# First two token groups of an attention + two-MLP kernel: passes with rounded weights first, passes with their rests second, and a new written order

## The chip, the cores and the metric

The kernel runs on one core of one Trainium2 chip. The metric is the device time of one launch in microseconds (us). Five engines run side by side, each through its own list of instructions in order: TensorE (PE: matmuls), VectorE (DVE), ScalarE (ACT), GpSimd (POOL) and SyncE (SP, which here issues every transfer). They wait for each other through semaphores only.

## The reference, cut to what matters

```python
attn_out = softmax(where(s >= max(s) - tau, s, -1e9)) @ v       # s = q k^T / 8; 4 x 8 heads, 576 x 64
x = attn_out.transpose(0, 2, 1, 3).reshape(2304, 512)
h = x @ w_in                                                     # 512 -> 2048
g = (a0 + a1 h + a2 h^2 + a3 h^3) / (1 + |b0||h| + |b1|h^2 + 1e-6)
y = g @ w_out                                                    # 2048 -> 512
out = ((y @ w1) * (y @ w2) @ w3) @ w_out2                        # 512 -> 1024 -> 1024 -> 512
```

All inputs and the output are float32, and `moe_b` is scaled up by 47.694.

## The kernel before, in words

**Tiling.** Tokens are worked on in 18 groups of 128: group n < 16 is block n % 4 of batch n // 4, groups 16 and 17 hold the last 64 rows of two batches each. Attention goes by batch b, head pair c and 128-row block (`qk`, `top`, `thr`, `exp`, `recip`, `p_norm`, `p_hi`, `p_lo`, `p_t`, `pv`, `x_split`). `p_t` is a transposing transfer through SP, and `pv` multiplies its result with V.

**Split numbers.** A float32 operand of the MLPs is carried as two float16 numbers: the rounded number (the first half of a tile) and the rest that the rounding left (the second half). A product takes three passes for each of its four weight pieces, in the code (0,0), (0,1), (1,0): rounded times rounded, and each rounded number times the other's rest. So a product of 128 tokens with 512 columns is 12 matmuls of 128x512, issued in two halves of 6: pieces 0 and 1, then pieces 2 and 3. The four products are `h_product` (w_in), `y_product` (w_out), `ab_product` (w1, w2) and `o_product` (W = w3 @ w_out2, made once by `w_product`).

**Weight preparation.** Each of 72 raw tiles of 512 KB is loaded (`raw_w`) into one of three `wr` buffers, turned into float32 words in two steps (`conv_w`: the head by any engine, then a shift and an or on DVE, which frees the buffer), squared on ACT for a norm (`square_w`, `norm_w`), and split: `split_w` writes the rounded piece from ACT, DVE or POOL, PE makes the rest in PSUM (two matmuls against `dg`, one against `minus`), and ACT or DVE copies it out.

**Scales.** `limits` loads tau and derives the factor of q and the threshold; `powers` loads the coefficients a and b and takes a logarithm and an exponential of one number on ACT; `setup` selects the one table of ACT functions that holds everything the kernel needs, and sets a few constants.

**The order.** All events (2533 calls like "qk of batch 0, head pair 1, block 2") are made into generators. `ORDER` is a long string of 3944 tokens that says which generator is advanced next, on which engine its copy runs (a for ACT, p for POOL, v or nothing for DVE), and into which buffer numbers its tiles go. Every engine's list of instructions follows from that string, and nothing is reordered later. The line in the loop is `if gens[n] is not None: next(gens[n], None)`, so each `yield` in a function is a place where other work can come between.

**Names that the prediction uses.** L410 to L434: `limits` and `powers`; L398: the table of `setup`; L451, L452, L408, L670: loads of q, k, tau and weights; L681: second step of `conv_w`; L512/L507: `qk`; L521: `top`; L359: `thr` and the like; L543/L548: `exp`; L599: `pv`; L688/L691: squares; L697: `norm_w`; L733/L734: the matmuls that make a rest; L809: `h_product`; L930: `w_product`.

Of the kernel before, what the change touches and what calls it, by code (L numbers as in the profile page):

```python
# [32 lines left out]
52.0 36.1 0 38a.0 38.0 14.0.1 1 15v 54p.1 54.1 8.0 3 23.0.1 28.2 2 25.0 27 29v.0 31.0.2 33.3 33a  # L33
31a 30a.0 30.2 4.1 51.1.0 5.0.0 35a 48.0 50p.1 35 37v 45v.4 10.1 6.2 7.1 50.3 53.1 55 9.0 44.2 47
11.1 12 12.0 12 84a.0.0 19.5.6 46p.0 46.4 21a 84 32.0 86.7.8 57v.1 34v.1 34.5 16.2 13v.1.1 13 20.0
40.1 49.0 59.1.0 62.1 18v.0 39v.3 88a 18.6 24.2 41p 152a.2.2 62a 152 59a 64a 64 90.0.1 74a.2 22v.1
66a 92.2 94 42a.0 76 96p.2 68p.4 98.2.1 70p 43.1 78 22.7 61.0 56.1 26v.1 98a 100.0 100a 119.0.1
26.8 72 56 75.2 63p.1 42.9 102a 102 113v.3 115 121.3 56 123 125a.0 104a 107v.2 127.3.5 127a 129.6
129a 63.10 65.1 103.0 80.0.0 109v 82v 77a.0 77.11 158.0.1 56 82 111.0 116.2 117.1 118a.1 160.0
67p.0 67.12 162 164v.1 131v 131 141v.0 133v 58v.13 105p.0 166.4.4 154.1.2 166a 143 69.0 105.14  # L40
118.15 69 168.6 17v.3.3 17 69 168a 170a 135a.3 156p 186.0.1 188.1 137v 170 180a.7 106.1 69 190
79.0 81v.0 108v.1 81.16 120.2 71a.17 172v 139 108.18 174v.8 145 192p.2 195.5.5 132.0 83.1 197.3
122v.0 83 182 93.1 184.2 195a 122.19 621.2 176v 147.0 149v 149 197a 223.0.1 199p 199 225.2 201v
203a.0 134p.1 134.20 89.0 227 229v.0 95a.0 178.0 95.21 205p 91v.1 231.6.6 231a 83 83 110.0 110
233.4 233a 252.0.1 91.22 254.3 110 171.1 85a.23 219.7.5 221p 97.1 209v.8 256 97 97 97 288 647.0
650p.0 136.0 624v.1 235p 624.24 258v.1 641.2 173a.1 211 260.7.1 262.2 173.25 262a 235 645v.1
246a.3 213 124.1 650.26 110 99v.27 260a 237v 163.0 290.1.0 645.28 112v.29 652.1 126p.0 291.0
165v.1 126.30 293 295a.2 297.0.8 297a 207 298.0 298a 148.2 165.31 150p.0 613.0 140.1 613 142a.1
628.0 150.32 264p 179.2 248 630p.0 264 300v 652 314.1.0 316.1 142.33 613 652 250.1 613 318 300
630.34 319p.0 321.1.4 321a 240v.5 242v 210.1 212p.1 339.1 302a 266v 274v.3 155.0 616a.35 309a.6  # L50
276 181v.0 212.36 181.37 633.0 114.1 311 284.7.2 633 157a.1 268v.0 157.38 278 619.1 128.1 304a.3
341.2 342v.1 218.1 220p.0 305v 323.8 270v 194.2 196p.1 633 633 636a.39 652 323a 187.0 344.2.1
220.40 226.1 196.41 215.0 217v 234.2 655a.42 189p.0 130.1 60.1 344v 346p 217 325a 144.1 286a
189.43 228p.1 236p.0 202.0 365 138 151.0 325 326v 146 159.1 153 153 167.0 161.0 169 191.1 228.44
193.1 204p.1 183.0 241.1 236.45 244.0 175.1 177 185 185 367.0.1 312.2 198.1 200 327.2 204.46 206.0
346 369.3 370 272 333v.5 335 208 243p.0 222.1 224.0 230.0 238.1 313.0 243.47 328p.6 330p 372v.2
320.1 232 239 214.0 216 216 245.1 247 247 249 249 329p.1 374.3.8 251p.0 267v.48 376.4 263v.49 376a
348a 349p.0 315p.0 255a.50 265a.51 253a.52 280.1 253.0 257a.53 337 329.54 259v.55 281a.56 374a
438.0 438 277a.3 659.0 282v 315.1 255.1 255a 285.2 438 438 377p 261a.10 391.1.0 438 253a 287a.1
257.1 377 393.0 259.0 307.0 287.12 257a 277.1 382.0 73.1 259a 332 282 267.0 351p 269p.11 386v.5  # L60
379a 322v.0 283a.16 277a 395 397v.0 441.0 267a 271v.14 398.4.1 400.2 638.0 322.22 261.1 292.2
362.3.6 398v 385p.1 388 261a 385.21 347.1 101.1 294p.0 400v 334.0 87.0 363a 390.1 263.0 263v 661
294.18 368.2 350v.1 381p.4 350.15 441 265.1 443.0 299.1 443.1 265a 443.0 273a.28 387.0 448p 450
445 269.0 450 416.1 336p.0 445 418.1 419v.1 421.5.7 358.1.1 336.19 383v 338.0 384.0 459.0 452.0
353.5 421a 423p 452 459 275v.6 402a 461.1 461.0 452 452p 360a 461.1 402 371v.1 375.0 301a.0 269v
273.1 360 301.7 273a 460.0.1 317.1 404a 405p.8 352.1 340.1 458 466v 468 423 271.0 271a 371.2
279a.8 275.1 462.2 407p 324.1 463 411a.4 464 468 275v 464 373.1 465a.2 355.1 343a.0 303.1 467.6.0
# [24 lines left out]
543.0 526v 543 526 558.0 634.7 823.0 875.1 632a 594.1 634a 578.0 809.1 656.0.1 597 594 746v.42 594
832.1 834 561 899.22 594v 579v.6 581p 596.2 809a 620p 658.1 885.0 660 935.1 663p.1 746.1 583 598a
854.1 843.0 846 858 911a.1 858 860 860 746a 600a.1 524 561 750.1 877a.0 637a 637 580 522 602p
863v.23 863 649a.5 651 750a 803.1 665.4.0 668.4 604.7 665a 935 877.44 668a 889a.0 580 599 1143.1
599 671p 671 889.17 682a.6 803v 880.0 601.1.0 892.1 806.1 776.1 883.0 911.54 601 603a 812v.21 806a
654.2 894 530 603 703.0.1 706.3 812.1 606.2 914.0 673a 685 639a 609.1 699.1.5 708 903.1 711p.0
812a 611a 866v.26 866 611 610 906 916 916 868v.1 868 713.6.4 920 713a 702a 872v.20 687 920 1185.3
605.1 872 716.7 1166.0 716a 607a 785.0.1 1166 607 612.0 642p.6 643p 933 719p 646.0 788.2 790
675a.8 677v 1191.1 1171a.0 793v.2 795.0.0 795a 1191 925v.19 1194.0 1072.2 1194 1196a.1 778v.3.3  # L100
719 1152.1 778 925 923v.17 797.6 923 1199 935 797a 737.0.1 740.0 742 799p 720a 680 694.1 1149.0
723a.8 1149 1199p.1 730a.2 1199p 1155a.1 745a.1 725p 1152 697a.0.0 935 928v.44 728.1 733 928 1157
799 1157v.0 1157p 747.7.3 749.4 780.7.8 931a.22 931 1168.0 1160.1 1207.1 1207 1202.0 749a 747a
782a 751p 935 1168 819.1.0 751 1174 754a 1210.0 1213v.1 1210 811a.1 821.1 824 825a.0 614.1 608 814
# [177 lines left out]
def tile_attention_mlps(  # L282
# [16 lines left out]
    nc = tc.nc  # L299
# [3 lines left out]
    KD = 4  # L303
# [495 lines left out]
    def h_product(n, f):  # L799
# [4 lines left out]
        for c in range(KD):  # L804
            if c == 2:
                yield
# [433 lines left out]
```

## Time and profile before

| | |
|---|---|
| median of 3 runs | 1009.08 us (1007.95 to 1009.59) |
| profiled execution | 1012.52 us, its span (first to last instruction) 1010.7 us |
| PE busy | 956.4 us, 95% of the span |
| DVE, ACT, POOL busy | 787.9, 668.6, 330.4 us |
| mean granted TensorE clock | 0.985 |
| bytes moved | 153.32 MB, mean 152 GB/s |

A busy PE is not a PE at its peak: a 128x512 float16 matmul has a mean row of 379 ns on the page, but twelve in a row take 2.59 us in the chain of waits, 216 ns from one to the next. Shares of busy time over the whole span hide the stages: PE is idle for some 45 us in the first 185 us and for about 5 us in all that follows, up to its last matmul.

### The profile page before, as it was taken

To read this page: it belongs to the slowest core of one execution; us is meant where nothing else is said; L and a number is where in the kernel's file an instruction comes from. 1 tells how busy PE (TensorE), PEld (TensorE's weight loads), DVE (VectorE), ACT (ScalarE), POOL (GpSimd) and SP (SyncE) were. 2 spreads that over 40 slices of the span, in tenths; PEclk is the share of its full clock that TensorE was granted. 3 is DMA by queue.
4 is the path that set the end of the run, shared out by engine and by line. 5 is a ranking of instruction groups with operands and counts; after the bars stand their busy time and mean duration, and the time that the engine had idled before them with its cause. 6 is when DMAs were issued, how large, how long until landed. Compare 5 with 4: busy or idle time off the path is not lost.

```text
span 1010.7 us, 15534 instructions
## 1 busy us (share of the span) xinstructions
PE 956.4 (95%) x5260; PEld 461.2 (46%) x5260; DVE 787.9 (78%) x1540; ACT 668.6 (66%) x1259; POOL 330.4 (33%) x366
## 2 busy tenths in 40 slices
PE   2689887999999999999999999999999999999998
PEld 1344343444444545544445454544544444444443
DVE  4766799988888898988688889998878665875732
ACT  4644699988777878877767877887665435554400
POOL 1212344333234435335334334324143123121310
PEclk9989888999999999999999999999999999999999
DMA  7988899789965777995757776875737465333243
GB/s 254 249 217 248 243 243 244 184 220 198 202 137 123 153 153 163 164 197 110 144 110 175 143 155 162 155 164 111 136 91 123 89 117 116 51 63 73 44 73 73
DMA packets 334047, 153.32 MB, mean 152 GB/s; under 512 B 307344, under 2 KB 311440, under 8 KB 333968
## 3 DMA queue, kind: packets, MB, share of 16 engines
q1 hardware_dynamic: 333968, 152.34, 68.2%
q8 instruction: 41, 0.67, 0.3%
q14 instruction: 38, 0.31, 0.1%
HBM read 68.67 MB, written 8.13 MB: 76 GB/s over the span
## 4 chain that ended last, share of the span: by engine, by line
PE 68%; DVE 5%; DMA 4%; ACT 3%; issue 1%; POOL 1%; SPq 1%; DVEq 0%; ACTq 0%; POOLq 0%
PE y L873 15%; PE h L809 15%; PE h L980 10%; PE y L1009 8%; PE S L980 6%; PE S L512 5%; PE h L599 4%; PE y L733 3%; DMA gt<-gg 3%; PE S L507 1%; DVE m L521 1%; PE y L734 1%; DMA x<-gg 0%; SPq L584 0%; DVE U L829 0%
## 5 line engine op out<-in xcount | busy, mean ns | idle before, releaser
L873 PE MATMUL y<-wp,gt 128*128 128x512 f16 x864 | 199.4, 379 | 2.0 <-DMA gt<-gg 1.0
L809 PE MATMUL h<-wp,xp 128*128 128x512 f16 x768 | 178.0, 380 | 1.1 <-DVE U L831 0.5
L980 PE MATMUL h<-wp,yy 128*128 128x512 f16 x576 | 132.1, 379 | 1.1 <-DMA yy<-d_y 0.9
L873 PEld LDWEIGHTS <-gt 128*128 128x128 f16 x864 | 83.1, 98 | 106.0 <-issue 6.8
L521 DVE TENSOR_REDUCE m<-S 128x1 f32<-128x576 f32 x144 | 104.8, 750 | 18.4 <-PE S L512 17.6
L809 PEld LDWEIGHTS <-xp 128*128 128x128 f16 x768 | 73.8, 98 | 95.9 <-issue 11.4
L512 PE MATMUL S<-raw 64*128 64x288 f32 x512 | 90.1, 451 | 27.7 <-ACT p L548 17.4
L352 POOL TENSOR_TENSOR A<-A,r 128x512 f32<-128x512 f32 x51 | 65.6, 1288 | 111.9 <-ACT r L824 106.6
L1009 PE MATMUL y<-wp,gt 128*128 128x512 f16 x432 | 100.4, 379 | 0.3 <-DMA gt<-gg 0.3
L543 ACT ACTIVATE S<-S,th 128x576 f32<-128x576 f32 x124 | 85.7, 708 | 21.6 <-DVE th L359 11.8
L817 ACT ACTIVATE U<-h,cf 128x512 f32<-128x512 f32 x72 | 55.9, 776 | 64.5 <-PE h L809 41.4
L980 PEld LDWEIGHTS <-yy 128*128 128x128 f16 x624 | 59.7, 98 | 76.8 <-issue 6.3
L548 ACT ACTIVATE p<-S,xy 128x576 f32<-128x576 f32 x124 | 91.2, 740 | 2.7 <-DVE hl L349 0.2
L352 POOL TENSOR_TENSOR hl<-p,hl 128x576 f16<-128x576 f32 x48 | 65.3, 1360 | 63.4 <-ACT hl L336 32.3
L352 POOL TENSOR_TENSOR gg<-A,r 128x512 f16<-128x512 f32 x39 | 52.4, 1344 | 102.3 <-DVE A L852 51.7
L512 PEld LDWEIGHTS S<-raw 64*128 64x128 f32 x512 | 49.8, 195 | 64.3 <-ACT p L548 25.8
L829 DVE SCALAR_TENSOR_TENSOR U<-h,cf,U 128x512 f32<-128x512 f32 x72 | 53.5, 746 | 24.4 <-ACT r L824 18.7
L839 ACT ACTIVATE r<-A,lnb 128x512 f32<-128x512 f32 x72 | 51.8, 719 | 30.6 <-POOL A L352 22.9
L848 DVE SCALAR_TENSOR_TENSOR gg<-U,cf,r 128x512 f16<-128x512 f32 x72 | 53.9, 749 | 20.0 <-ACT r L841 13.9
L681 DVE SCALAR_TENSOR_TENSOR cw<-rw,head 128x512 int32<-128x512 int32 x72 | 52.0, 725 | 17.0 <-ACT head L336 13.5
L1009 PEld LDWEIGHTS <-gt 128*128 128x128 f16 x432 | 41.5, 98 | 51.8 <-issue 2.5
L930 PE MATMUL h<-cw 128*128 128x512 f32 x128 | 60.4, 625 | 0.6 <-DVE cw L681 0.6
(202 smaller groups left out, 1642.2 us busy)
## 6 DMA issues: line engine op xcount, KB each, us to landing
rw<-in_moe_w_dram SPq DMA_DIRECT2D x32, 511.8 KB, 4.5
rw<-in_moe_w_out_dram SPq DMA_DIRECT2D x24, 511.8 KB, 4.6
raw<-in_k_dram SPq DMA_DIRECT2D x32, 288.0 KB, 3.4
rw<-in_moe_w_in_dram SPq DMA_DIRECT2D x16, 511.8 KB, 4.4
wr<-in_v_dram SPq DMA_DIRECT2D x13, 576.0 KB, 4.6
out_dram<-A SPq DMA_DIRECT2D x16, 256.0 KB, 2.3
wr<-in_v_dram SPq DMA_DIRECT2D x12, 320.0 KB, 3.4
d_y<-x SPq DMA_DIRECT2D x13, 256.0 KB, 2.3
```

The lines of the kernel that those rows point to most:

```text
L352: (nc.gpsimd if eng[0] == "p" else nc.vector).tensor_tensor(o, x, y, op=op)
L512: nc.tensor.matmul(t[s][:, half, :HS], x[r, o:o + 128], y[r, keys], start=True, stop=True)
L521: nc.vector.tensor_reduce(st["m", b, c, blk][:, s:s + 1], t[:, :, :HS], axis=AX.XY, op=ALU.max, negate=True)
L543: nc.scalar.activation(t, t, AF.Prelu, bias=th, alpha=BIG)
L548: nc.scalar.activation(x, t, AF.Exp, bias=xy[:, 0:1], accum_out=su)
L809: nc.tensor.matmul(t, x[:, y, c, o:o + 128], w[:, a, :], start=c + i == 0, stop=c == KD - 1 and i == 2)
L817: nc.scalar.activation(u, h, AF.Identity, bias=cf[:, 15:16], scale=cf[:, 0:1])
L848: stt(p[:, 0, :], u, cf[:, 3:4], r, ALU.add, ALU.mult)
L873: nc.tensor.matmul(st["y", n], x[:, 4 * a + j, :], w[:, y, :], start=f + j + i == 0, stop=f == 3 and j == 3 and i == 2)
L930: nc.tensor.matmul(t, st["cw", ("w3", m, j // 4)][:, o:o + 128], st["cw", ("wo2", j)], start=j == 0, stop=j == 7)
L980: nc.tensor.matmul(t, x[:, 4 * y + c, :], w[:, a, :], start=c + i == 0, stop=c == KD - 1 and i == 2)
L1009: nc.tensor.matmul(st["o", n], x[:, 4 * a + j, :], w[:, y, :], start=hf + j + i == 0, stop=hf == 1 and j == 3 and i == 2)
```

## The change: what it does

For the groups n = 0 and n = 1, all four products now issue in their first half the two passes of each of the four pieces that use the rounded weight (8 matmuls), and in the second half the one pass of each piece that uses the weight's rest (4 matmuls). The other groups keep 6 and 6. `split_w` puts a weight tile into the table of tiles before its rest is written, so that a product may be issued between the two. The string `ORDER` is replaced as a whole: the 2533 events and the 3944 tokens are the same in number and kind, in another order, with other engines for some copies and other buffer numbers.

```diff
 ORDER = """
-52.0 36.1 0 38a.0 38.0 14.0.1 1 15v 54p.1 54.1 8.0 3 23.0.1 28.2 2 25.0 27 29v.0 31.0.2 33.3 33a
...
@@ split_w
         t = T(tag, [128, 2, 512], F16, name="wp")
         copy(t[:, 0, :], r, scale)
+        st["w", key] = t
         yield
         if key[0] == "w12" and key[2]:
             rest(t[:, 1, :], r, t[:, 0, :], scale)
-            st["w", key] = t
             return
...
         copy(t[:, 1, :], y)
-        st["w", key] = t
@@
+    def halves(n, rests):
+
+        p = ((0, 0), (0, 1), (1, 0))
+        if n >= 2:
+            return [[(c, q) for c in (0, 1) for q in p], [(c, q) for c in (2, 3) for q in p]]
+        return [[(c, q) for c in range(4) for q in p if q != rests], [(c, rests) for c in range(4)]]
+
     def h_product(n, f):
 
         t = st["h", n, f] = P("h", [128, 512])
         x = st[x_of(n)]
         o = 128 * (n % 2) if n < 4 * B else 0
-        for c in range(KD):
-            if c == 2:
+        for k, half in enumerate(halves(n, (1, 0))):
+            if k:
                 yield
-            w = st["w", ("in", f, c)]
-            for i, (a, y) in enumerate(((0, 0), (0, 1), (1, 0))):
-                nc.tensor.matmul(t, x[:, y, c, o:o + 128], w[:, a, :], start=c + i == 0,
-                                 stop=c == KD - 1 and i == 2)
+            for c, (a, y) in half:
+                nc.tensor.matmul(t, x[:, y, c, o:o + 128], st["w", ("in", f, c)][:, a, :],
+                                 start=k + c + a + y == 0, stop=k == 1 and (c, (a, y)) == half[-1])
...
```

`y_product`, `ab_product` and `o_product` are changed in the same way. Lines behind L727 move down by a few (L809 becomes L814, L930 becomes L935).

The next rows are of ACT, from its first instruction. `c`, `aa`, `bb` belong to `limits` and `powers`, `head` to `conv_w`, `S` and `p` to `exp`. Before:

```order
L398 ACT_TABLE_LOAD
L336 ACTIVATE head_102<-rw 128x512
L410 ACTIVATE c_86<-tau_t 128x1
L421 ACTIVATE aa<-pa 128x4
L422 ACTIVATE bb<-bb 128x2
L427 ACTIVATE c_93<-c_86 128x1
L428 ACTIVATE c_93<-c_93 128x1
L543 ACTIVATE S<-S,th 128x2x288 x2
```

ACT in the change, at the same place:

```order
L410 ACT_TABLE_LOAD
L410 ACTIVATE c_86<-tau_t 128x1
L421 ACTIVATE aa<-pa 128x4
L422 ACTIVATE bb<-bb 128x2
L427 ACT_TABLE_LOAD
L427 ACTIVATE c_93<-c_86 128x1
L428 ACT_TABLE_LOAD
L428 ACTIVATE c_93<-c_93 128x1
L398 ACT_TABLE_LOAD
L336 ACTIVATE head_102<-rw 128x512
L336 ACTIVATE head_103<-rw 128x512
L543 ACTIVATE S<-S,th 128x2x288
```

`setup` now comes behind `limits` and `powers`, and ACT's list holds four table loads instead of one; the first `head` stands behind the last of them.

The next rows are of DVE, around the second threshold (`th<-m`, of batch 0, pair 0, block 1) and the scaling of V (`vs`, `vh`, `vl`). Before:

```order
L521 TENSOR_REDUCE m<-S 128x1 x2
L349 SCALAR_TENSOR_TENSOR hl<-p,su,hl 128x576
L474 TENSOR_REDUCE vs<-vs 128x1
L439 TENSOR_SCALAR vs<-h 128x1
L440 TENSOR_SCALAR vs<-vs 128x1
L441 TENSOR_SCALAR vs<-vs 128x1
L443 TENSOR_SCALAR vs<-vs 128x1
L681 SCALAR_TENSOR_TENSOR cw<-rw,head_102 128x512
L349 SCALAR_TENSOR_TENSOR vl<-pT,vs,vh 128x640
L359 TENSOR_SCALAR th<-m,c_86 128x2
```

DVE in the change:

```order
L521 TENSOR_REDUCE m<-S 128x1
L359 TENSOR_SCALAR su<-su 128x2
L563 RECIPROCAL su<-su 128x2
L342 TENSOR_SCALAR p<-p,su 128x576
L521 TENSOR_REDUCE m<-S 128x1
L359 TENSOR_SCALAR th<-m,c_86 128x2
L349 SCALAR_TENSOR_TENSOR hl<-p,su,hl 128x576
L474 TENSOR_REDUCE vs<-vs 128x1
```

The threshold now stands right behind its second `top`, ahead of the work on V.

The last rows are of PE, from its first instruction: `S` is `qk`, `h<-cw` is `w_product`, `h<-pT` is `pv`. Before:

```order
L512 MATMUL S<-raw 128x288 x8
L477 MATMUL h<-vs,c_86 128x1
L512 MATMUL S<-raw 128x288 x4
L930 MATMUL h<-cw 128x512 x2
L512 MATMUL S<-raw 128x288 x4
L930 MATMUL h<-cw 128x512 x4
L599 LDWEIGHTS vh
L599 MATMUL h<-pT,vh 64x256
...
```

PE in the change:

```order
L512 MATMUL S<-raw 128x288 x8
L477 MATMUL h<-vs,c_86 128x1
L512 MATMUL S<-raw 128x288 x8
L935 MATMUL h<-cw 128x512 x2
L599 LDWEIGHTS vh
L599 MATMUL h<-pT,vh 64x256
...
L935 MATMUL h<-cw 128x512 x4
```

The fourth `qk` now stands ahead of the first quarter of `w_product`, and the first `pv` ahead of its second and third quarters.

## Rows read from the trace of the kernel before

**Rows 1.** Page, part 1: busy us (share of the span) and instructions of each engine.

```profile
PE 956.4 (95%) x5260; PEld 461.2 (46%) x5260; DVE 787.9 (78%) x1540; ACT 668.6 (66%) x1259; POOL 330.4 (33%) x366
```

**Rows 2.** Stretches: us, then busy us (instructions) by engine, clock, DMA share, GB/s.

```profile
0.00:60.82 60.82, 30.79 (x107) 15.32 (x107) 36.30 (x77) 30.25 (x62) 12.81 (x22) 0.98 0.88 252
60.82:116.02 55.20, 55.20 (x193) 25.89 (x193) 38.82 (x70) 27.20 (x53) 14.80 (x18) 0.96 0.83 235
116.02:129.79 13.77, 8.68 (x26) 2.69 (x24) 10.94 (x19) 9.46 (x18) 6.49 (x10) 0.75 0.93 227
...
184.56:1005.93 821.37, 816.22 (x4722) 394.86 (x4721) 650.31 (x1263) 547.75 (x1009) 272.01 (x290) 1.00 0.64 132
```

**Rows 3.** Waits of PE, first 200 us: us in total, times, longest.

```profile
PE S L512 <- ACT p L548: 17.4, 8, 6.7
```

**Rows 4.** Instructions in order of time, 0 to 14 us: start, us, engine, line.

```profile
0.72 1.28 ACT L398 ACT_TABLE_LOAD   x1 [0.72 <-PEq L1227]
...
5.91 0.77 ACT L336 ACTIVATE head<-rw 128x512 f16<-128x512 bf16 x1 [3.91 <-POOL minus L415]
6.71 0.69 DVE L681 SCALAR_TENSOR_TENSOR cw<-rw,head 128x512 int32<-128x512 int32 x1 [5.87 <-ACT head L336]
...
9.12 0.35 DVE L342 TENSOR_SCALAR raw<-raw,flag 128x256 f32<-128x256 f32 x1
...
9.53 2.29 PE L512 MATMUL S<-raw 64*128 64x288 f32 x8 [9.53 <-DVE raw L342]
...
11.44 0.21 ACT L421 ACTIVATE aa<-pa 128x4 f32<-128x4 f32 x1 [2.44 <-DMA pa<-in_moe_a_dram]
...
13.15 0.75 DVE L521 TENSOR_REDUCE m<-S 128x1 f32<-128x576 f32 x1
```

**Rows 5.** DMA issues, 0 to 40 us: count, KB each, median us to landing.

```profile
rw<-in_moe_w_dram SPq DMA_DIRECT2D x4, 511.8 KB, 4.9
pT<-in_v_dram SPq DMA_DIRECT2D x3, 576.0 KB, 7.2
raw<-in_k_dram SPq DMA_DIRECT2D x3, 288.0 KB, 5.0
...
raw<-in_q_dram SPq DMA_DIRECT2D x3, 128.0 KB, 4.7
```

**Rows 6.** Instructions in order of time, 26 to 45 us.

```profile
27.00 1.34 ACT L543 ACTIVATE S<-S,th 128x576 f32<-128x576 f32 x2 [0.75 <-DVE th L359]
...
30.69 3.01 PE L512 MATMUL S<-raw 64*128 64x288 f32 x8 [6.70 <-ACT p L548]
...
33.62 1.72 PE L930 MATMUL h<-cw 128*128 128x512 f32 x2
...
38.61 1.28 SPq L584 DMA_TRANSPOSE pT<-hl  x1
...
40.34 3.70 PE L930 MATMUL h<-cw 128*128 128x512 f32 x8
...
43.97 1.17 PE L599 MATMUL h<-pT,vh 128*64 128x256 f16 x18
```

**Rows 7.** PE in order of time, four places from 57 to 144 us.

```profile
57.19 0.75 PE L512 MATMUL S<-raw 64*128 64x288 f32 x2 [2.25 <-ACT p L548]
...
60.82 7.76 PE L930 MATMUL h<-cw 128*128 128x512 f32 x12
...
99.47 5.42 PE L930 MATMUL h<-cw 128*128 128x512 f32 x12
...
143.99 1.46 PE L809 MATMUL h<-wp,xp 128*128 128x512 f16 x6
```

**Rows 8.** The stretch 129.79 to 176.76 us, columns as in rows 2.

```profile
129.79:176.76 46.97, 37.97 (x197) 18.81 (x196) 44.43 (x99) 45.49 (x99) 21.00 (x24) 0.87 0.98 244
```

**Rows 9.** Its ACT groups by line: names, shapes, count, busy us, mean ns.

```profile
L691 ACT ACTIVATE sq<-cw 128x512 bf16<-128x512 f32 x16 | 10.2, 644 | 0.0
L338 ACT ACTIVATE wp<-cw,wsc 128x512 f16<-128x512 f32 x10 | 6.8, 716 | 0.0
```

More of the change, by code (lines that the diff above doesn't have):

```diff
@@ L38 @@
[L38 to L43, printed above, removed]
@@ new lines @@
+923 778 675p.0 677p 1078.1 646.0 680 612.2 793a.2 608 1188 795.7.4 719p 719 1191 795a 797.1 797a
+1194.1 1196v.1 720a 935 1194 1199 737.1.0 1149.0 928a.14 928 1149 1152.1 694.0 740.0 1152 742
+1199p.0 730a.5 723a.7 1199v 1202.2 725v 1155v.1 931v.20 728.2 1207.0 1207 615a.0.0 733 1157
+1157a.1 931 745v.0 747.0.0 749.2 747a 925v.37 925 1168.1 935 1168 1174 749a 751p 751 819.1.0
+780.6.7 799p 754a 1210.1 1157v 1213a.1 756p.3 1210 821.1 782a 759v 697a.2.2 762 1160.0 824 1216
+825p.1 799 811v.8 1174a.0 814 828.1.0 1174v 828a 1177.1 831.1 614.0 831a 614 689.0.1 764v.3 618.0
@@ new lines @@
+1979.1.0 1714.3.0 1714 1820p 1716a 1981.2 1905 1822 1845.1 2251.0 1822 2251 1859 1859 1716 1983
+2253.1 1984a.0 1940.1 1958 1960a 2253 1986.3.5 1986a 2248.1 1988.1 1824.1 2248 1988a 1824 1824
+1719.2 1723 2256v.1 1824p 1827.2 2259 1912.0 1861.0 1990v 2004.1.0 1861 1861 1990 1829 2259p.1
+2006.3 1898.1 1913a 1967a.2 1898 2008 1913 1942a.3 1879.0 1879 1944 1992a 1968 2259p 1945.0
+2009p.2 2011.2.4 2011a 1861p 1900.0 2270.0 1961v.8 1963v 1900.0 1721 1900.0 1902 1829 1847 1847
+1882.1 2261.0 1882.1 1970 2013.6 1884 1882.1 1999p.3 2264 1965 2000 2264 2013a 1976.2.1 1886v
@@ L278 @@
+2498 2474 2519 2498 2344 2526.1 2526 2527 2475a.1 2480p.1 2499v.1 2500 2520.0 2480p 2520 2481.0
+2521 2521 2522a.0 2523 2476 2500a.1 2482.1 2482 2488 2488 2489v.0 2527 2495.2 2523a.0 2523p 2500p
+2528v.0 2529 2501.0 2489 2529a.1 2524.1 2529v 2496.0 2496 2530.2 2502 2502 2503v.0 2525.1 2475
+2525 2503 2531 2531 2532a.1 2532
 """
@@ L867, in y_product @@
         x = st.pop(("turned", ("g", n, f)))
-        for j in range(4):
-            if j == 2:
+        for k, half in enumerate(halves(n, (0, 1))):
+            if k:
                 yield
-            w = st["w", ("out", 4 * f + j)]
-            for i, (a, y) in enumerate(((0, 0), (0, 1), (1, 0))):
-                nc.tensor.matmul(st["y", n], x[:, 4 * a + j, :], w[:, y, :], start=f + j + i == 0,
-                                 stop=f == 3 and j == 3 and i == 2)
+            for j, (a, y) in half:
+                nc.tensor.matmul(st["y", n], x[:, 4 * a + j, :],
+                                 st["w", ("out", 4 * f + j)][:, y, :], start=f + k + j + a + y == 0,
+                                 stop=f == 3 and k == 1 and (j, (a, y)) == half[-1])
     def y_norm(n):
@@ L974, in ab_product @@
         x = st["turned", ("y", n)]
-        for c in range(KD):
-            if c == 2:
+        for k, half in enumerate(halves(n, (1, 0))):
+            if k:
                 yield
-            w = st["w", ("w12", which, hf, c)]
-            for i, (a, y) in enumerate(((0, 0), (0, 1), (1, 0))):
-                nc.tensor.matmul(t, x[:, 4 * y + c, :], w[:, a, :], start=c + i == 0,
-                                 stop=c == KD - 1 and i == 2)
+            for c, (a, y) in half:
+                nc.tensor.matmul(t, x[:, 4 * y + c, :], st["w", ("w12", which, hf, c)][:, a, :],
+                                 start=k + c + a + y == 0, stop=k == 1 and (c, (a, y)) == half[-1])
         if which and hf:
@@ L1003, in o_product @@
             st["o", n] = P("y", [128, 512])
-        for j in range(4):
-            if j == 2:
+        for k, half in enumerate(halves(n, (0, 1))):
+            if k:
                 yield
-            w = st["w", ("W", 4 * hf + j)]
-            for i, (a, y) in enumerate(((0, 0), (0, 1), (1, 0))):
-                nc.tensor.matmul(st["o", n], x[:, 4 * a + j, :], w[:, y, :],
-                                 start=hf + j + i == 0, stop=hf == 1 and j == 3 and i == 2)
+            for j, (a, y) in half:
+                nc.tensor.matmul(st["o", n], x[:, 4 * a + j, :], st["w", ("W", 4 * hf + j)][:, y, :],
+                                 start=hf + k + j + a + y == 0,
+                                 stop=hf == 1 and k == 1 and (j, (a, y)) == half[-1])
     def o_scale(n):
```

467 lines of the change are left out of this document (229 added, 238 removed).

## The prediction

> **What bounds the kernel now.** I read the page first, then busy time by stages, then PE's waits, and at the end the instructions in order of time at the places where the order was changed. The page says that PE is busy for 956.4 of 1010.7 us [rows 1], so some 54 us could be won if PE never stood still. The stages say where they are [rows 2]: up to 60.82 us PE is busy for only 30.79, so 30.0 us are idle; from 60.82 to 116.02 it is busy throughout; from 116.02 to 129.79, while the norms of w_in are taken, 5.1 us are idle; and from 184.56 to its last matmul at 1005.93 only 5.15 of 821.37. Behind 184.56 the time is thus PE's own work, which the change leaves alone in kind and number, and nothing there can give more than those 5.15 us. What an order can win or lose is decided ahead of that point. The list of waits says by what: PE's longest total is 17.4 us, eight times, a `qk` that wants an S buffer that ACT's exponential has not yet read [rows 3].
>
> One stage needs a second look. From the last norm at 129.79 to the `qk` of batch 0, pair 2, block 4, at 176.76, ACT is busy for 45.49 of 46.97 us and DVE for 44.43, PE for 37.97 [rows 8]. There ACT sets the pace, and PE waits for it at the end. What counts in this stage is how many steps of ACT stand ahead of that `qk`.
>
> **The change part by part.** I sum against the profiled execution, 1012.52 us with a span of 1010.7, and carry the difference over to the median of the runs, 1009.08, which is 3.4 lower.
>
> The *passes* themselves: 12 matmuls stay 12 matmuls with as many weight loads, 8 and 4 instead of 6 and 6. What they can win is a wait of PE for a weight's rest. The first `h_product` begins at 143.99 with no idle time ahead of it [rows 7], so there is no such wait to take away; in the new order its two halves even stand back to back, behind all four rests. I count 0 for them. No reason is seen for a loss, so the bound on that side is 0; on the other the new halves let PE do two more matmuls early, 2 of the 6 that take 1.46 us, 0.5 us each time, and only where PE would stand still, so no more than 2 us in all.
>
> The *start*. The change loads q, k and tau first, then one weight tile, then a and b; before, two tiles and one V tile of 576.0 KB went ahead of a and b. By [rows 5] that is 2016 KB ahead of them before and 928 KB now, 1088 KB less, and at 252 GB/s [rows 2] 4.3 us; they landed at 11.44 [rows 4], so now at about 7.1. But behind them ACT has to go through its new list: two small steps (0.2 each), three table loads of 1.28 with two small steps between them, and a `head` of 0.77 [rows 4], 5.4 us together: 12.5. DVE's list is in order, and the scaling of the first q (0.35) now stands behind the small steps of `powers` and behind the `cw` (0.69) that needs that `head`. So the first `qk` starts at 12.5 + 0.69 + 0.35 = 13.5, against 9.53: 4.0 us late. Behind the waiting `cw` on DVE also stands the release of a weight buffer, so SP, in order, holds the loads of the fourth weight tile and of three V tiles until about 13 and later.
>
> What is late next? Before, the first `top` came at 13.15 [rows 4], because DVE had to finish `powers` first; that is done by now, so of the 4.0 us 1.4 are given back at once (the `qk` ends at 11.82 before). The second threshold, in its new place, comes right behind its `top` and not behind the scaling of V; before, ACT stood ready and waited for it until 27.00 [rows 6]. I place the second exponential at 25 to 27 and the third `qk` at 30 to 31, where it was (30.69). So the start costs 0 at this point, with bounds of -2 and +4.0.
>
> *pv and the fourth qk moved ahead.* The first `pv` ran at 43.97, as its last transposed tile, issued at 38.61, had just landed; before it PE did two quarters of `w_product`, 3.70 us from 40.34 [rows 6]. In the change these stand behind `pv`, and the first quarter (33.62) stands behind the fourth `qk`. If the tile lands when it did, the 3.70 us come after it and not before it. The bounds are 0 (the tile lands so early that PE never waits) and +5.4 (3.70 and the 1.72 of the first quarter). I take +3.0, near the 3.70 and a little under it, since the tile's own steps stand somewhat further forward on DVE.
>
> *What gives it back.* Behind this PE still stood still for 2.25 us at 57.19, for 0.72 and 0.27 in two smaller waits, 3.24 in all, and the twelve `w_product` matmuls from 60.82 took 7.76 us where the same twelve from 99.47 took 5.42 [rows 7]; the clock of the stretch from 60.82 is 0.96 on the mean [rows 2], which hides a part at 1.2 instead of 2.4 GHz behind the idle time ahead of it. With its work pushed back by 3 us PE arrives later at the same `qk`, and the wait is eaten up: -3.2. Of the 2.3 us of slow clock I take a third back, -0.7, between 0 and -2.3.
>
> *The norms of w_in.* 39 weight tiles are loaded ahead of the last one of w_in in both orders; I count 0, with a bound of one tile either way, 511.8 KB [rows 5] at 227 GB/s [rows 2], 2.3 us.
>
> *The stage that ACT bounds.* From the last square of w_in up to and with the exponential that frees the buffer of that `qk`, I count 76 program steps on ACT before and 76 in the change. Two squares (0.64) fewer and two rounded pieces (0.72) more [rows 9], and the like in small: less than 0.3 us. The engines changed elsewhere, but here ACT has the same load, so the stage takes as long: 0, bound 1 either way. That is where the gain of the new order would have to be seen.
>
> *Behind 184.56*: 0, between -5.15 (all idle time gone) and +2 (a few turned tiles late). The last eight half products stand back to back in both orders.
>
> The sum: 0 + 0 + 3.0 - 3.2 - 0.7 + 0 + 0 + 0 = -0.9 us: 1011.6 for a profiled execution like this one, 1008.2 for the median.
>
> A rule that speaks against the change: the row of the table load has 1.28 us, and nothing of ACT follows until 5.91 [rows 4], so up to 3.9 us behind it could be spent unseen. The Trainium skill ("ScalarE: Activation LUTs", section "What ACT_TABLE_LOAD costs") gives the same 1283 ns for the load and adds about 1380 ns of drain for each switch to another set; by that page three more switches would be 8.0 us and not 3.85, and an estimate of the first `qk` would be near 17.6. The trace agrees on the load and cannot tell on the drain, as only one load is in it.
>
> **The rivals.**
>
> *A, the forecast:* the start's delay is taken up, the order wins as much as it loses: 1008.2, own range 1006 to 1010.5.
>
> *B, pv does not hold PE:* the fourth `qk` and the transposes come a few us earlier, the +3.0 falls away and the rest stays: -3.9, 1005.2. For it: the second threshold no longer waits for V, and q and k are loaded first. Against it: `cw` and `head` at the start are late, and the weights for `w_product` with them.
>
> *C, the table loads reach the end, slower than before:* the 3.6 us that the three loads (3.85) add, less what the earlier a and b give, come through to the PE-bound stage. PE is busy without a gap from 60.82 to 116.02, so a delay that is still there at 60.82 is paid in full. It decides from about 3.2 us of delay, the idle time between 46 and 59 that can take it up: -0.9 + 3.6 = +2.7, 1011.8. For it: SP's loads of V hang behind the same buffer, and `pv` needs V. Against it: 30 us of idle time ahead.
>
> *D, each switch takes twice its row:* a tail as long as the row itself behind each load, 3 x 1.28 = 3.85 more on ACT at the start, within the 3.9 that the trace leaves open; with the slack used up it goes through: -0.9 + 3.85 = +2.95, 1012.0. The page above would make it 4.1 instead.
>
> *E, the change doesn't do what it says:* the passes bring nothing as PE never waited for a rest. This is part of A, which counts 0 for them.
>
> **How the numbers follow.** Chances: A 0.42, B 0.30, C 0.18, D 0.10. 0.2% of 1009.08 is 2.0 us, about what a measurement of this kernel can tell from no change; so faster is below 1007.1 and slower above 1011.1. Of A 0.30 is the same, 0.08 faster (some of the 5.15 behind 184.56), 0.04 slower; of B 0.27 faster, 0.03 the same; of C and D 0.22 slower, 0.06 the same. That makes 0.35, 0.39 and 0.26. The range from 1004.0 to 1012.8 holds B with 1.2 below it, and D with 0.8 above.
>
> **What would show it right or wrong.** First `qk` of PE at 13 to 14 us, four table loads on ACT; the third `qk` at 30 to 31.5; `pv` with a wait for a transposed tile near 43, and `w_product` behind it; no idle time from about 48 to 60; ACT busy for 97% from the last norm to the `qk` of pair 2, block 4, in a stretch of 46 to 48 us; PE's idle time behind that at 4 to 7 us. It is wrong if the first `qk` comes by 10 us (the loads are hidden), if PE's gapless part begins more than 2 us away from 60.8, or if the ACT-bound stage is more than 2 us shorter, since then the order has won there what I did not find.

## The result, and the profile after

The changed kernel takes 1016.39 us, the median of four runs (1014.38 to 1017.36), beside 1009.24 for the kernel before on the same chip: a ratio of 1.0058, interval [1.0032, 1.0084]. Timed again it was 1015.89 beside 1010.1, 1.0061 [1.0041, 1.0081]. That is 6 to 7 us slower, where 1008.2 was forecast.

The stretches of the profile after, with the columns of [rows 2], against [rows 2, 8]:

```profile
0.00:63.60 63.60, 31.91 (x102) 15.30 (x102) 38.92 (x81) 34.50 (x64) 11.14 (x19) 1.00 0.82 244
63.60:115.37 51.77, 50.97 (x170) 23.41 (x169) 35.89 (x57) 30.91 (x62) 14.59 (x20) 1.00 0.86 241
115.37:130.31 14.94, 9.16 (x51) 3.47 (x52) 9.73 (x19) 10.87 (x22) 3.77 (x7) 0.77 0.81 213
130.31:179.33 49.02, 37.17 (x197) 18.34 (x196) 45.83 (x102) 45.99 (x97) 23.16 (x24) 0.92 0.92 233
179.33:186.34 7.01, 6.97 (x18) 3.25 (x19) 4.71 (x10) 6.88 (x17) 3.48 (x5) 0.61 1.01 294
186.34:1009.40 823.06, 816.74 (x4728) 395.41 (x4727) 640.04 (x1238) 559.66 (x1020) 300.15 (x310) 1.00 0.65 132
```

The stage from the last norm to the `qk` of pair 2, block 4, is 49.02 us and not 46.97. ACT is busy in it for 45.99 us and not 45.49, as the count of its steps had said; what grew is its idle time, 3.03 us instead of 1.48. Behind the stage PE is idle for 6.3 us instead of 5.15. PE at the start, after:

```profile
41.76 3.00 PE L512 MATMUL S<-raw 64*128 64x288 f32 x8 [6.22 <-DVE p L546]
44.68 3.76 PE L935 MATMUL h<-cw 128*128 128x512 f32 x4
48.37 1.17 PE L599 MATMUL h<-pT,vh 128*64 128x256 f16 x18
...
50.02 3.70 PE L935 MATMUL h<-cw 128*128 128x512 f32 x8
...
70.05 1.24 PE L512 MATMUL S<-raw 64*128 64x288 f32 x8
```

Before, at the last of these places:

```profile
70.16 1.24 PE L512 MATMUL S<-raw 64*128 64x288 f32 x8
```

After its wait of 6.22 us for the fourth `qk`, at 41.76, PE has no idle time until 115.37; before, waits of 0.27, 2.25 and 0.72 us still came behind that `qk`. So in these two profiles the changed kernel catches up: the `qk` of pair 3, block 0, starts at 70.05, and at 70.16 before. From them alone the start costs nothing and the stage 2 us. But their spans are 3.5 us apart and the medians 6 to 7: the profiled execution of before was itself 3.4 us above its median. The experiments had to find out what it had lost.

ACT's start after, to be read against [rows 4]:

```profile
0.72 1.28 ACT L410 ACT_TABLE_LOAD   x1 [0.72 <-PEq L1231]
...
7.76 0.20 ACT L421 ACTIVATE aa<-pa 128x4 f32<-128x4 f32 x1 [2.56 <-DMA pa<-in_moe_a_dram]
8.09 0.20 ACT L422 ACTIVATE bb<-bb 128x2 f32<-128x2 f32 x1
8.31 1.28 ACT L427 ACT_TABLE_LOAD   x1
9.61 0.20 ACT L427 ACTIVATE c<-c 128x1 f32<-128x1 f32 x1
9.83 1.28 ACT L428 ACT_TABLE_LOAD   x1
11.12 0.20 ACT L428 ACTIVATE c<-c 128x1 f32<-128x1 f32 x1
11.34 1.28 ACT L398 ACT_TABLE_LOAD   x1
12.63 1.40 ACT L336 ACTIVATE head<-rw 128x512 f16<-128x512 bf16 x2
```

Four loads as foreseen. Behind the second, third and fourth the next activation starts 0.01 to 0.02 us after the load ends: no drain shows. (Behind the first ACT waits 3.00 us for tau.) The first `qk` starts at 14.46.

### The profile page after: what moved, and what is told of

Read it like the earlier page. It is cut to its first block, busy times and chain, and to the rows that moved or that the text cites. A ratio compares the mean times of both kernels' runs of the same rounds, so it can differ in the third digit from the quotient of the medians.

```text
span 1014.2 us, 15565 instructions
## 1 busy us (share of the span) xinstructions
PE 953.0 (94%) x5260; PEld 459.2 (45%) x5260; DVE 775.1 (76%) x1504; ACT 689.5 (68%) x1280; POOL 356.3 (35%) x384
## 5 line engine op out<-in xcount | busy, mean ns | idle before, releaser
L814 PE MATMUL h<-wp,xp 128*128 128x512 f16 x768 | 179.4, 382 | 2.7 <-ACT wp L336 1.4
L814 PEld LDWEIGHTS <-xp 128*128 128x128 f16 x768 | 74.2, 99 | 98.0 <-issue 11.6
L352 POOL TENSOR_TENSOR gg<-A,r 128x512 f16<-128x512 f32 x44 | 60.4, 1373 | 160.8 <-DVE A L857 83.3
L352 POOL TENSOR_TENSOR hl<-p,hl 128x576 f16<-128x576 f32 x52 | 68.6, 1322 | 23.4 <-ACT hl L336 13.6
L853 DVE SCALAR_TENSOR_TENSOR gg<-U,cf,r 128x512 f16<-128x512 f32 x72 | 56.5, 788 | 20.5 <-ACT r L846 14.5
L349 DVE SCALAR_TENSOR_TENSOR hl<-p,su,hl 128x576 f16<-128x576 f32 x64 | 55.4, 867 | 9.0 <-ACT hl L338 6.2
L826 ACT ACTIVATE A<-h,cf 128x512 f32<-128x512 f32 x72 | 48.9, 682 | 16.7 <-DVE U L836 10.3
```

The source lines that it names most:

```text
L349: nc.vector.scalar_tensor_tensor(o, x, scale, hi, op0=ALU.mult, op1=ALU.subtract)
L352: (nc.gpsimd if eng[0] == "p" else nc.vector).tensor_tensor(o, x, y, op=op)
L814: nc.tensor.matmul(t, x[:, y, c, o:o + 128], st["w", ("in", f, c)][:, a, :], start=k + c + a + y == 0, stop=k == 1 and (c, (a, y)) == half ...
L853: stt(p[:, 0, :], u, cf[:, 3:4], r, ALU.add, ALU.mult)
```

## The experiments

Ratios are to the kernel before, timed in the same round of experiments; medians of different rounds are less comparable than these ratios. Three columns come from each kernel's one profile, between events that all orders have: the start of the `qk` of pair 3, block 0 (A), the time from there to the `h_product` of group 0, quarter 3 (B), and from there to PE's last end (C).

| kernel | median, us | ratio [95%] | A | B | C |
|---|---|---|---|---|---|
| before, as shown | 1009.08 | | 70.16 | 114.40 | 821.37 |
| r_before | 1008.91 | 0.9993 [0.9969, 1.0018] | 71.33 | 114.34 | 820.50 |
| changed, as shown | 1016.39 | 1.0058 [1.0032, 1.0084] | 70.05 | 117.15 | 822.27 |
| r_after | 1015.89 | 1.0061 [1.0041, 1.0081] | 68.57 | 117.40 | 822.55 |
| e1_setup_first | 1014.49 | 1.0050 [1.0031, 1.0070] | 70.21 | 115.11 | 822.01 |
| e2_old_order_new_passes | 1010.69 | 1.0013 [0.9999, 1.0026] | 66.01 | 114.28 | 822.21 |
| e4_new_order_old_passes | 1015.62 | 1.0059 [1.0040, 1.0077] | 69.26 | 117.31 | 821.23 |
| h1_after_head_before_tail | 1013.80 | 1.0038 [1.0020, 1.0056] | 69.72 | 115.32 | 822.05 |
| h2_before_head_after_tail | 1014.04 | 1.0053 [1.0034, 1.0072] | 66.98 | 117.01 | 823.82 |
| e5_table_first | 1012.92 | 1.0038 [1.0023, 1.0053] | 66.72 | 116.06 | 822.55 |
| e6_before_with_four_loads | 1014.54 | 1.0052 [1.0035, 1.0069] | 73.78 | 114.42 | 821.84 |
| s1_three_steps_off_scalar | 1013.77 | 1.0043 [1.0027, 1.0060] | 67.00 | 117.24 | 823.17 |
| s2_engines_of_before_in_stage | 1027.01 | 1.0193 [1.0164, 1.0222] | 66.36 | 129.71 | 823.30 |
| h3_before_to_185_after_tail | 1017.19 | 1.0083 [1.0063, 1.0103] | 65.37 | 114.04 | 830.47 |
| s3_stage_order | 1013.53 | 1.0043 [1.0029, 1.0057] | 66.70 | 116.65 | 823.79 |
| h6_after_head_and_stage | 1014.53 | 1.0050 [1.0030, 1.0069] | 67.72 | 117.58 | 822.80 |
| h3b_before_to_183_after_tail | 1010.20 | 1.0004 [0.9990, 1.0019] | 65.84 | 114.72 | 824.41 |
| b1_before_conv_behind_exp | 1008.50 | 0.9985 [0.9971, 0.9999] | 64.17 | 114.46 | 821.04 |
| h7_after_stage_alone | 1012.52 | 1.0041 [1.0026, 1.0056] | 67.26 | 116.97 | 822.87 |
| h8_first_part_of_stage | 1013.85 | 1.0049 [1.0030, 1.0068] | 64.59 | 119.99 | 823.63 |

### Passes or order

r_after is the changed kernel again.

> The changed kernel as it is, timed again beside the kernel before. All theories expect +6 to +8 us against the kernel before (the ratio 1.006 to 1.008). Its profile is a second one of the same program: the lag behind the profile of before, taken at equal work of TensorE, should again be within 0.5 us of zero from 70 to 118 us, +1 to +2 us at the first split of w_in (about 135 us) and +2 to +4 us from 180 us on. A lag of 5 us or more at 100 us would speak for the start.

The ratio came as expected. The lag did not: A is 68.57, 1.6 us ahead of the profile of before and not within 0.5 us of it.

e2 has the changed functions under the old string:

```diff
-14.0.1 1 52.0 3 36.1 28.2 8.0 0 54a.0
+52.0 36.1 0 38a.0 38.0 14.0.1 1 15v
...
```

> The order of the kernel before with the new split of the passes for the first two token groups (rounded weights of all four pieces in the first half, rests in the second). Theory 'passes' (the split itself costs, by its accumulation order or its waits): slower than before by 2 us or more, 1011 us or more. Theories 'stage' and 'tables', for both of which the order is the cause: within 1 us of the kernel before, 1008 to 1010 us.

e4 has the old functions under the new string, two first halves moved behind the rests they read:

```diff
-... 478.1 (step 554) ... 478 (593) ... 513 (890)
+... 478.1 478 (592, 593) ... 513 (903)
```

> The order of the changed kernel with the passes of before; since these need the rests of the first two pieces in the first half, two steps of 2533 are put later: the first half of the first product of group 0, third quarter, and the first half of the output product of group 0, fourth quarter, each behind the rest it reads. Theory 'passes': near the kernel before, 1008 to 1011 us. Theory 'order' (stage or tables): as slow as the changed kernel or up to 1 us slower, 1015.5 to 1018 us; if the early first half made TensorE wait in the stage of the splits, up to 1.5 us faster than the changed kernel, 1014.5 us.

e2 is at 1.0013, e4 at 1.0059: the loss goes with the order, and 'passes' falls; by e2's interval, up to 1.0026, they cost 2.6 us at most. Only those two products of the new order used the freedom at all. One gained nothing by it. PE in order of time in the changed kernel: the early half stands at 158.85, the second half still waits for a rest at 166.94, and the next `qk` waits for ACT.

```profile
158.85 1.90 PE L814 MATMUL h<-wp,xp 128*128 128x512 f16 x8 [0.90 <-DVE xp L349]
...
166.94 0.81 PE L814 MATMUL h<-wp,xp 128*128 128x512 f16 x3 [1.37 <-ACT wp L336]
...
172.00 2.07 PE L512 MATMUL S<-raw 64*128 64x288 f32 x8 [2.62 <-ACT p L548]
```

### The start

e1 was meant to load one table. The token moved was 2, which is `diagonals`, and not 0, `setup`:

```diff
-14.0.1 1 52.0 3 36.1 28.2 8.0 0 54a.0 ... 155.0 2 264
+2 14.0.1 1 52.0 3 36.1 28.2 8.0 0 54a.0 ... 155.0 264
```

> The changed kernel with its one step setup put first again, so that ScalarE loads its function table once and not four times; all else is the same. Theory 'stage' (the loss arises between 115 and 180 us, where ScalarE and TensorE take turns on the weights' pieces): the first product of q and k starts by about 10 to 11 us and not at 14.5, and the end moves by less than 1 us, 1015.5 to 1017 us. Theory 'tables' (the three more table loads reach the end): 3.5 to 5 us faster than the changed kernel, 1011.5 to 1013 us.

ACT still loads four tables and the first `qk` is at 14.65, so it tells nothing of the loads. e5 does it rightly, and e6 puts the four loads into the kernel before:

```diff
-14.0.1 1 52.0 3 36.1 28.2 8.0 0 54a.0
+0 14.0.1 1 52.0 3 36.1 28.2 8.0 54a.0
```

```diff
-52.0 36.1 0 38a.0 38.0 14.0.1 1 15v 54p.1 54.1 8.0 3
+52.0 36.1 14.0.1 1 8.0 3 0 38a.0 38.0 54p.1 54.1 15v
```

> The changed kernel with the step that names the function table put first, so that ScalarE loads one table and not four (the earlier try moved another step, which makes a matrix, and left the four loads). Theory 'start by tables': the first product of q and k at 10.5 to 11.5 us in place of 14.5, and 2.5 to 3.5 us faster than the changed kernel, 1012.5 to 1013.5 us. Theory 'start by its order' (the start is later because of where the heads' steps stand, the tables hide): first product early but the third within 1 us of the changed kernel's, and the end within 1 us, 1015 to 1017 us.

> The kernel before with its first twelve steps in another order: the step that names the table behind the limits and the powers, and the scaling of the first q behind both, so that four tables are loaded; nothing else is moved. Theory 'start by tables': the first product at about 14.5 us, and 2 to 4 us slower than before, 1012 to 1014 us. Theory 'start by its order' or 'stage': within 1 us of before, 1009 to 1011 us.

With one load the first `qk` is at 11.29 and A at 66.72; over the five profiles with the changed first steps A is 69.6 on the mean, over the five with the table first 66.9. The ratio falls from 1.0061 to 1.0038, 2.3 us (3.0 by the medians, which come from two rounds); with intervals of 1.5 to 2 us each way that alone would not be clear of noise, but the A of the two groups do not overlap (68.57 to 70.21, and 66.36 to 67.72). In the kernel before, the same twelve steps cost 5.2 us, ratio 1.0052 [1.0035, 1.0069], more than the 2 to 4 expected; its first `qk` is at 17.46, since a lands later too (ACT's first use at 10.32, in the changed kernel at 7.76). So the start does reach the end: e6 shows it by time, and h1 will. h1 joins the changed first 200 steps to the rest of before, h2 the reverse:

```diff
 ORDER = steps 1 to 200 of the change      (h2: of before)
+        then what is left, in the order of before   (h2: of the change)
```

> The first 200 steps of the changed order (to the product of q and k of pair 3, some 70 us of 1010), then all the rest in the order of the kernel before, with the passes of before; buffer places are given anew where two tiles would meet. Theory 'start' (the later start does reach the end, and the profiled execution of before hid it since it had itself lost 4 us to an idle stretch and a half clock between 55 and 66 us): slower than before by 2.5 to 4.5 us, 1012.5 to 1014.5 us. Theory 'stage' (the loss is all in the stage of 115 to 180 us): within 1 us of before, 1009.5 to 1011 us.

> The other half: the first 200 steps of the order before, then the rest in the changed order with the changed passes. Theory 'start': what is left is the stage's part, slower than before by 1 to 3 us, 1011 to 1013 us. Theory 'stage': the whole loss, 5 to 7 us slower than before, 1015 to 1017 us. The two halves should add to the loss of the changed kernel, about 6 us.

h1 gives 1.0038, as 'start' says; h2 1.0053, in neither window. The two add to 9 us and not 6; with intervals of 2 us each way that is a loose fit and no proof of the parts.

### What the profile of before had lost

r_before is the kernel before again.

> The kernel before again, for a second profile of the same program. Theory 'start': its first gapless stretch of TensorE begins 3 to 4 us earlier than in the profile that the prediction read (the product of q and k of pair 3 at 66 to 67 us and not 70.16), with no stretch at half clock between 57 and 66 us, as in the other runs with the same first steps. If it is at 70 us again, the later start of the changed kernel cost nothing, and the two experiments with the table loads need another reading.

It did not come as expected: A is 71.33, and by these words that speaks against 'start'. But this execution took 1012.76, and the other seven of the same kernel 1007.54 to 1010.06: both profiles of this kernel fell on dear executions, some 3.5 us above the median. That was seen afterwards. For it speak the six other profiles with before's first steps, whose A is 64.6 to 67.3 (66.0 on the mean). What the two dear ones share is in [rows 7] and here, PE in r_before:

```profile
50.16 7.13 PE L930 MATMUL h<-cw 128*128 128x512 f32 x16
58.47 0.75 PE L512 MATMUL S<-raw 64*128 64x288 f32 x2 [1.18 <-ACT p L548]
59.94 2.28 PE L512 MATMUL S<-raw 64*128 64x288 f32 x6 [0.72 <-ACT p L548]
62.15 2.07 PE L930 MATMUL h<-cw 128*128 128x512 f32 x2
```

The six `qk` matmuls in e2:

```profile
57.50 1.23 PE L506 MATMUL S<-raw 64*128 64x288 f32 x6 [0.72 <-ACT p L542]
```

In r_before PE waits for an exponential, and then six `qk` matmuls take 2.28 us where the same six take 1.23 in e2, and two `w_product` matmuls 2.07: the granted clock is 0.50 from 59.94 to 66. Ahead of that, ACT in the profile of before:

```profile
46.49 0.77 ACT L336 ACTIVATE head<-rw 128x512 f16<-128x512 bf16 x1
54.94 0.78 ACT L336 ACTIVATE head<-rw 128x512 f16<-128x512 bf16 x1 [7.69 <-DMA rw<-in_moe_w_dram]
55.59 0.68 ACT L543 ACTIVATE S<-S,th 128x576 f32<-128x576 f32 x1
56.31 0.74 ACT L548 ACTIVATE p<-S,xy 128x576 f32<-128x576 f32 x1
...
57.04 0.70 ACT L543 ACTIVATE S<-S,th 128x576 f32<-128x576 f32 x1
57.77 0.74 ACT L548 ACTIVATE p<-S,xy 128x576 f32<-128x576 f32 x1
```

A weight's conversion stands ahead of two `exp` of two steps each in ACT's list and waits 7.69 us for its load. It waits there, 5.2 to 8.9 us, in every profile with before's first steps (in h7 and h8 the profile names a step of DVE as what ended the wait, in the other six the load). What differs is when it can start, and A mostly goes with that:

| profile | the conversion starts, us | the six `qk` matmuls take, us | A |
|---|---|---|---|
| h8 | 52.30 | 1.23 | 64.59 |
| h3 | 53.05 | 1.23 | 65.37 |
| h3b | 53.27 | 1.23 | 65.84 |
| h7 | 53.73 | 1.97 | 67.26 |
| e2 | 53.77 | 1.23 | 66.01 |
| h2 | 54.41 | 1.23 | 66.98 |
| before | 54.94 | 2.23 | 70.16 |
| r_before | 56.22 | 2.28 | 71.33 |

In the two latest, and for a part in h7, the slow clock comes on top. b1 moves the conversion behind the two `exp`:

```diff
-... 58v.13 118a.1 160.0 ... 105.14 118.15 69 168.6 ... 168a 170a
+... 58v.13 160.0 ... 105.14 69 168.6 ... 168a 118a.1 118.15 170a
```

> The kernel before with one conversion of a weight tile (its half on ScalarE and its half on VectorE) moved behind the four exponentials of pair 2, block 0, which stood behind it in ScalarE's queue while it waited 7.7 us for its load. Theory 'uneven start': TensorE's idle time between 55 and 59 us goes, and with it the half clock to 66 us; the fourth pair's product starts at 65 to 67 us in every profile, and the median is 0.5 to 2 us lower than before's, 1007 to 1009 us, with the slow executions (1011 us and more) gone. Rival: something else (the load itself) holds the stretch, and the median stays within 0.5 us.

PE in b1 at the same place:

```profile
49.48 5.31 PE L924 MATMUL h<-cw 128*128 128x512 f32 x12
54.73 1.24 PE L506 MATMUL S<-raw 64*128 64x288 f32 x8
55.90 5.42 PE L924 MATMUL h<-cw 128*128 128x512 f32 x12
```

No wait, no half clock, A at 64.17 (a little under the 65 to 67 expected), and 0.9985 [0.9971, 0.9999]: some 1.5 us faster than before, the lowest ratio here, though the interval all but reaches 1. Its twelve times end at 1010.44; of the 29 of before beside it eight are above 1010.5. That the waiting conversion is a cause of the uneven start is shown by the eight profiles and b1's; that it is the only one is not, and the time that the move gains is known only roughly.

### The stage from 115 to 185 us

Four steps are given to other engines in s1, 28 in s2, and two are moved in s3, all on top of e5:

```diff
-328a.3 ... 363a ... 381a.6 ... 356a.0
+328p.3 ... 363p ... 381p.6 ... 356v.0
```

> The changed kernel with the table named first, and in the stage of the first weights' splits four steps on other engines: two rounded halves of p (pair 0, block 3; pair 1, block 2; 0.67 us each on ScalarE) and the scaling of one q to GpSimd, one tail's split to VectorE. Theory 'ScalarE bounds the stage' (its busy time plus its waits is the stage's length): the stage ends 1.3 to 2.2 us earlier than with the table first alone, 1010.7 to 1011.7 us. Rival 'VectorE or the order of the splits bounds it': within 0.5 us of the kernel with the table first, 1012.4 to 1013.4 us.

> The changed kernel with the table named first, and all 28 steps of the stage (steps 380 to 640) that the change gave to another engine given back to the engine they had before; the order stays changed. Theory 'engines': the stage's loss of some 2 us goes, 1010.5 to 1011.5 us. Theory 'order' (the sequence of the splits, and what stands ahead of them on TensorE and SP, makes the loss): within 0.7 us of the kernel with the table first, 1012.2 to 1013.6 us.

```diff
-327.1 365 169 272 ... 391.0.1 251v.0 255.0 253a.3 253.1
+272 327.1 365 169 ... 251v.0 255.0 253a.3 253.1 391.0.1
```

> The changed kernel with the table first and two steps of the stage moved: on SP's queue the transposed tile of pair 3 goes ahead of the load of the weights' piece that held it up, and on TensorE the product of q and k of pair 1, block 3, goes behind the first two splits. Theory 'stage order': TensorE's wait of 2.7 us for the transposed tile falls to 1.5 us or less, the first split starts 1.5 to 2.3 us earlier (near 131.5 us), and the end comes 0.8 to 2 us earlier than with the table first alone, 1010.9 to 1012.1 us. Rival: the gain is eaten by ScalarE's and VectorE's work in the same stage, and the end stays within 0.5 us of 1012.9 us.

None helps. s1 takes 1.5 us from ACT between A and the end of B (90.18 busy, 91.68 in e5), and B grows by 1.2: 'ScalarE bounds the stage' falls in this form. s2 costs some 15 us: these engines don't fit this order, so 'engines' or 'order' stays undecided. In s3 PE's wait ahead of the turned tile's `pv` did go, 2.70 us in e5 (first row), 0.58 in s3 (second):

```profile
129.15 2.13 PE L594 MATMUL h<-pT,vh 128*64 128x256 f16 x18 [2.70 <-DMA pT<-hl]
```

```profile
127.60 2.13 PE L594 MATMUL h<-pT,vh 128*64 128x256 f16 x18 [0.58 <-DVE acc L696]
...
131.41 2.08 PE L728 MATMUL y<-cw,dg 128*128 128x512 f32 x2 [0.61 <-DVE dg L714]
```

The first split came 2.1 us earlier (133.54 in e5), but runs at half clock, 2.08 us for two matmuls that take 1.12 in e5, and B was longer by 0.6: the gain was used up inside the stage.

Where the loss lies was then cut out by position: h3 joins at step 690, h6 and h3b at 685 with buffer numbers renamed so that the same tiles share a buffer as in the source, h7 and h8 put a middle piece of the change into before:

```diff
 h6   steps 1 to 685 of e5, then before
 h3b  steps 1 to 685 of before, then the change  (h3: 690)
 h7   steps 405 to 685 of the change, the rest of before  (h8: 405 to 580)
```

> The order of the kernel before for its first 690 steps (to about 184 us), then the changed order, with the changed passes. What is left of the loss behind the stage: by the lag curves of the profiles 0.4 to 1.5 us, 1009.8 to 1011.3 us. If the part behind 185 us cost more than 2.5 us, 1012 us or more, then start and stage explain less than I say.

> The changed kernel with the table first for its first 685 steps (start and stage, to about 183 us), then the order of before, with the changed passes throughout; no buffer place differs from its source's pattern. If the stage makes the remaining loss: 2 to 3.5 us slower than before, 1011 to 1012.5 us, as the kernel with the table first. If the loss lies behind 185 us: within 1 us of before, 1008.5 to 1010 us.

> The order of before for its first 685 steps, then the changed order, the changed passes throughout, with the tail's buffer places renamed so that none differs in pattern. If the stage makes the remaining loss: within 1.2 us of before, 1008.5 to 1010.5 us. If the loss lies behind 185 us: 2 to 3.5 us slower, 1011 to 1012.5 us. The jump of 6.6 us at 372 to 425 us of the exchange at 690 should be absent.

> The order of before, but for steps 405 to 685 (123 to 183 us), which stand in the changed order; the changed passes throughout. Theory 'stage': its length between equal work of TensorE is 58 to 59 us in the profile, as in the eight profiles with the changed order, and not 56 to 57, and the median is 1.5 to 3.5 us above before's, 1010.5 to 1012.5 us. Rival 'the start's order' (its steps leave the stage with more to do, as steps put off): within 1 us of before, 1008 to 1010 us.

> The same with steps 405 to 580 alone in the changed order (123 to 162 us). If the loss is made by the late first split and what stands ahead of it: as the stage alone, 1.5 to 3 us above before. If it is made behind (the early first half of the third product, the product of pair 2, block 3, waiting for its p): within 1 us of before, 1008 to 1010 us.

h3 is spoilt by its own seam: C is 8 us longer, most of it at one place. PE stands for 2.17 us ahead of 377.73, waiting for a turned tile, and for 0.86 soon after, and then runs at half clock (columns as in [rows 2]). That exchanged buffers made the tile late is likely, not shown; in h3b PE has no idle time from 370 to 386.

```profile
370.00:380.00 10.00, 6.97 (x58) 3.30 (x56) 5.30 (x11) 6.16 (x11) 3.11 (x3) 0.98 0.55 122
380.00:386.00 6.00, 6.00 (x16) 2.52 (x17) 3.46 (x9) 2.65 (x7) 2.39 (x2) 0.50 0.46 87
```

h3b, without that, is at 1.0004 [0.9990, 1.0019]: behind step 685 the change costs nothing that can be told. h7 is at 1.0041 [1.0026, 1.0056], 4.1 us for the stage alone. h8 is at 1.0049 with the first part of the stage alone (up to 162 us), more than expected; but its B, 119.99, is longer than that of any kernel with the whole changed stage but s2, so the return to the old order may cost something of its own, and where in the stage the loss is made stays open. h6, 1.0050, keeps it all, more than expected. B agrees: 114.0 to 115.3 in the eight profiles with before's stage (mean 114.5), 115.1 to 117.6 in the ten with the changed one (116.8). From A to the end of B, e2 and h7:

```profile
66.01:180.29 114.28, 98.98 (x394) 46.12 (x394) 94.60 (x189) 85.82 (x180) 44.98 (x52) 0.91 0.94 244
```

```profile
67.26:184.23 116.97, 100.55 (x393) 45.89 (x393) 93.39 (x188) 87.29 (x180) 44.15 (x52) 0.91 0.91 238
```

Of the 2.7 us PE is idle for 1.1 (16.4 against 15.3) and longer busy with the same matmuls for 1.6; in the pair after and before it is all idle time (18.5 us against 14.3). ACT's busy time does not go with B: 87.29 us in h7, 91.68 in e5, whose B is the shorter. Which of the 280 steps make it is open; the two most suspect moves were tried, and taking them back did not help.

## Why the prediction was wrong, by its steps

- *Passes, 0*: right, as far as e2 (1.3 us, -0.1 to 2.6) and e4 can tell. Rival E with it.
- *Start, first `qk` at 13.5, third at 30 to 31*: 14.46 and 30.82, but the second part of the third `qk` waited until 33.25. The loads of 1.28 us were in it, and rival D (each switch twice its row) is refuted by the rows at 8.31 to 12.63. In these rows the next activation begins 0.01 to 0.02 us after the load ends. The Trainium skill ("ScalarE: Activation LUTs", section "What ACT_TABLE_LOAD costs") has a drain of about 1380 ns per switch besides the load; the trace doesn't show it, and the first `qk` came 3 us ahead of the 17.6 that the estimate by that page gave.
- *pv and the fourth `qk`, +3.0*: the size was near, the reason not quite: the fourth `qk` itself came 4.1 us late (41.76), waiting 6.2 us for an exponential on DVE, and `pv` at 48.37 waited for no tile.
- *Given back, -3.2 and -0.7; then 3.4 taken off for the median*: the first step that failed. In the two profiles it is even right (A: -0.11). But the idle time and the slow clock that took the delay up were those of one dear execution, and the same 3.4 us were then taken off again as though they lay elsewhere. An ordinary execution of before has A at 66.0 on the mean, the changed kernel at 69.6: 3.6 us reach the PE-bound part, 2.7 of them by the table loads (66.9 without). That is rival C in mechanism, held at 0.18 and priced as though the idle time were there.
- *Norms and the stage that ACT bounds, 0, bound 1*: the second. The stage was 2.05 us longer in the pair, 2.3 over all profiles, 4.1 [2.6, 5.6] in time by h7. The count of 76 steps of ACT on either side was borne out, 45.49 and 45.99 us busy; the step from it, "so the stage takes as long", was not: ACT itself was idle for 1.5 us more, and s1 and h7 show that ACT's load alone does not set the length. What does is open.
- *Behind 184.56, 0 between -5.15 and +2*: right, 0.4 [-1.0, 1.9] by h3b.
- *Its signs*: no idle time from 48 to 60 and four loads came; the first `qk` (14.46), ACT's share of its stage (94% and not 97%) and the length of that stage (49.02) missed. PE's gapless part began at 41.76 and not near 60.8, which the prediction had named as a sign of being wrong.

2.3 (e5, by the ratios; 3.0 by the medians) + 4.1 (h7) + 0.4 (h3b) = 6.8, beside 6 to 7 measured. By the profiles' means it is 3.6 in A and 2.3 in B.

## What to carry to other kernels

A delay at the start was hidden here only by idle time that not every execution has. Where the profiled execution lies above the median, its waits and its half clock are not a reserve to charge a delay to, and the difference must not be taken off a second time. Name the function table in ScalarE's first instruction: here three functions that came ahead of it loaded a table each. Look for a step that waits for a load ahead of ready work in an engine's list: moving one such conversion gained some 1.5 us here, at the edge of what the runs can tell.

## What the runs showed of the hardware

- A short wait of TensorE is paid twice where the clock falls behind it: in h3, 3.03 us idle between 370 and 380 us are followed by 6 us at a granted clock of 0.50; in r_before waits of 1.18 and 0.72 us by 6 us at 0.50.
- Executions of one and the same program differ by several us (before: 1006.83 to 1014.3 in 29; h7: 1011.42 to 1013.74 in 6). In the eight profiles with before's first steps A goes with the moment at which one waiting conversion can start: 64.59 where that is 52.30, 71.33 where it is 56.22.
- Four table loads cost 1.28 us each; behind the three that are followed by ready work nothing more shows. Of the 3.85 us of three loads 2.7 are still there at the `qk` of pair 3, and 2.3 in the time of the whole kernel, by e5.
